# Where TensorE's unused products stand, and who adds x to the output: a planned attention and adapter kernel on one core

## Chip, cores and metric

The kernel runs on one core of a Trainium2 chip. The metric is the device time of one execution in microseconds (us). Five engines matter: TensorE (PE: matrix products, into PSUM only), VectorE (DVE), ScalarE (ACT), GpSimd (POOL) and SyncE (SP). The last two mainly issue the DMAs here. Each engine works through its own queue in order and waits on semaphores for the others.

## What is computed

The reference is a cosine-weighted linear attention followed by a mixture of eight low-rank adapters, of which each row takes two:

```
# q, k, v: 8 batches, 8 heads, 576 positions, 64 channels
phi(x) = concat(relu(x) * cos, relu(x) * sin)          # cos, sin by position
kv  = sum over s of phi(k)[s] (outer) v[s];  z = sum over s of phi(k)[s]
x   = (phi(q) @ kv) / (phi(q) @ z + 1e-6)              # then (4608 rows, 512)
logits = x @ w_gate;  top 2 of 8 experts;  w = softmax over the two
out = x + sum over the two e of w[e] * (x @ A[e]) @ B[e]
```

All inputs and the output are float32 in HBM; the kernel works in bf16 inside.

## The kernel before

**Tiling.** The 4608 rows of x are worked in 36 groups of 128 rows. A group is either 128 positions of one batch (kind "one", two j of 9) or one j of two batches (kind "two"). Batches go in four pairs; the last pair has nine groups of kind "two".

**Steps.** For each batch: load K, V and Q by DMA (`load`, L386; casting to bf16), relu of K (`relu_k`, L417), V scaled by cosine and by sine (`vscale`, L427: nine instructions on ScalarE, L434, or one on VectorE, L436), the product of K and V on TensorE (`kv_mm`, L439, 36 or 72 products, L447, into the PSUM tile pnd), and two evacuations of it into the block-diagonal tile BD (`kv_evac`, L454), one for each half of the partitions. For each group: transposes of q (`qt_mm`, L533), evacuation with relu on ScalarE (L539), times tangent on VectorE (`qt_tan`, L559), the num products (`num_mm`, L577, into pnd), a reciprocal of the denominators (L589) and the normalized tile xt (`x_xt`, L594). Then, for three groups at a time: transposes of xt (L603), their copy to SBUF (`xt_evac`), the product with A and the gate (`za_mm`, L616), the routing on VectorE and one sigmoid on ScalarE (L630 to L665), a transpose of the weighted result (L674) and its copy. The output tile of a group is summed in PSUM by two products (`dx_mm`, L682): xt times the identity (L685), which only carries x into the sum, and the routed result times B (L687). ScalarE or VectorE copies the sum to the tile osb (`osb`, L690, through `copy`, L241 or L243), and `store` (L695) sends it out from SP's or POOL's queue.

**Unused products.** TensorE also runs products whose result nobody reads. Two blocks of 18 stand at the start (`pe_warm`, L301). `pe_more` (L305 to L308) appends n products of 128x252 to a step: six to each half K·V step of batches 0 and 1 (L500) and four to the num step of the first five groups (L741), 44 in all. They write columns of pnd that the step itself leaves free.

**Order.** Nothing is scheduled at run time or by the compiler. Every step is entered in a plan (`Plan.add`) with its possible engines, their assumed costs, and the tiles that it uses. Four tables fix the rest: ORDER is the order in which all 594 steps are issued, and so each engine's queue; CHOICE picks the engine of each step; SLOTS picks the buffer of each use of a pool; HOLD makes a store wait for another DMA. Pools that matter: pnd has two buffers of two PSUM banks, shared by K·V and num; ps has four banks, shared by everything else on TensorE; osb has seven, of which the first two hold K of batch 0 at the start. The batch loads are all in POOL's queue. Waits between engines are put in by the framework, tile by tile, from what each instruction reads and writes.

Of the kernel before, what the change touches and what calls it, by code (L numbers as in the profile page):

```python
# [20 lines left out]
    26, 19, 32, 16, 20, 51, 15, 27, 14, 18, 0, 17, 1, 36, 2, 9, 29, 3, 12, 10, 52, 28, 33, 13, 31, 35, 4, 30, 11, 7,  # L21
    34, 5, 46, 37, 21, 6, 54, 50, 55, 38, 45, 39, 23, 8, 40, 44, 61, 114, 115, 41, 116, 22, 60, 125, 117, 42, 124, 43,
    126, 134, 70, 121, 127, 118, 53, 62, 122, 154, 119, 135, 120, 155, 145, 71, 144, 49, 123, 128, 69, 48, 299, 24,
    156, 131, 129, 47, 130, 298, 136, 132, 301, 133, 56, 146, 137, 79, 65, 302, 300, 57, 25, 78, 303, 58, 59, 355, 64,
    147, 141, 356, 138, 357, 360, 142, 358, 63, 80, 139, 140, 143, 304, 151, 359, 361, 305, 152, 66, 362, 88, 306, 73,
    373, 68, 74, 67, 363, 364, 148, 89, 160, 374, 161, 149, 375, 150, 171, 162, 170, 153, 307, 157, 172, 163, 308,
    376, 378, 164, 309, 158, 173, 87, 181, 159, 200, 377, 180, 201, 191, 165, 379, 166, 190, 182, 167, 380, 311, 192,
    174, 202, 183, 96, 381, 310, 72, 168, 175, 365, 169, 97, 369, 176, 177, 382, 178, 385, 193, 366, 75, 312, 179,
    107, 82, 386, 314, 393, 370, 77, 76, 313, 367, 315, 394, 187, 395, 398, 396, 184, 397, 81, 98, 83, 412, 185, 399,
    188, 186, 316, 189, 194, 400, 317, 203, 195, 413, 106, 196, 216, 217, 414, 417, 368, 197, 204, 415, 318, 416, 218,  # L30
    319, 320, 198, 418, 206, 199, 207, 321, 401, 205, 84, 105, 419, 402, 208, 219, 322, 387, 91, 383, 86, 323, 388,
    430, 209, 85, 392, 405, 384, 92, 210, 324, 420, 213, 211, 421, 406, 246, 403, 431, 247, 212, 226, 372, 227, 404,
    432, 236, 435, 90, 228, 237, 450, 433, 214, 248, 238, 93, 451, 215, 434, 452, 410, 407, 99, 95, 220, 453, 94, 455,
    229, 422, 408, 223, 221, 239, 454, 423, 424, 222, 426, 425, 390, 436, 224, 230, 437, 427, 326, 225, 438, 325, 231,
    439, 328, 456, 232, 329, 327, 233, 457, 444, 234, 330, 101, 429, 458, 440, 240, 459, 441, 235, 469, 445, 241, 446,
    100, 331, 332, 243, 333, 447, 262, 470, 263, 242, 253, 264, 252, 244, 272, 474, 471, 245, 273, 254, 102, 472, 265,
    473, 274, 255, 464, 462, 475, 110, 103, 389, 460, 463, 249, 428, 465, 476, 334, 335, 461, 250, 109, 477, 442, 478,
    466, 283, 336, 282, 487, 251, 443, 108, 479, 284, 337, 448, 488, 111, 275, 338, 492, 489, 285, 480, 483, 113, 411,
    490, 481, 104, 391, 491, 507, 112, 493, 494, 482, 256, 508, 484, 495, 509, 292, 257, 510, 486, 485, 496, 258, 259,
    293, 512, 501, 511, 260, 499, 261, 502, 266, 371, 513, 294, 500, 497, 514, 340, 506, 505, 267, 269, 268, 498, 467,  # L40
    515, 339, 270, 503, 342, 271, 341, 276, 504, 343, 344, 277, 279, 468, 516, 278, 526, 280, 281, 345, 286, 346, 527,
    347, 528, 287, 517, 529, 531, 288, 348, 449, 289, 530, 518, 543, 532, 290, 533, 349, 544, 519, 350, 291, 521, 520,
    548, 534, 545, 295, 546, 522, 535, 524, 523, 351, 547, 296, 538, 549, 352, 525, 550, 536, 409, 539, 297, 540, 537,
    551, 560, 552, 541, 353, 561, 555, 542, 354, 562, 565, 557, 563, 564, 553, 556, 566, 567, 579, 558, 554, 568, 569,
    580, 570, 559, 581, 584, 571, 582, 574, 583, 575, 572, 585, 589, 586, 573, 576, 577, 587, 588, 578, 590, 592, 591,
    593,
]
CHOICE = [
    0, 0, 0, 0, 0, 0, 0, 0, 0, 0, 0, 0, 0, 0, 0, 0, 0, 0, 0, 0, 0, 0, 0, 0, 0, 1, 0, 0, 0, 0, 0, 0, 0, 0, 0, 1, 0, 0,
    0, 0, 0, 0, 0, 1, 0, 0, 0, 0, 0, 1, 0, 0, 0, 1, 0, 1, 0, 0, 1, 0, 0, 0, 0, 0, 1, 0, 0, 0, 0, 0, 0, 0, 1, 0, 0, 0,  # L50
    0, 1, 0, 0, 0, 0, 0, 1, 0, 0, 0, 0, 0, 0, 0, 0, 0, 0, 0, 0, 0, 0, 0, 0, 0, 0, 0, 0, 1, 0, 0, 0, 0, 0, 0, 0, 0, 0,
# [4 lines left out]
    0, 0, 0, 0, 0, 0, 0, 0, 0, 0, 0, 0, 0, 0, 0, 0, 0, 0, 0, 0, 0, 0, 0, 0, 0, 0, 0, 0, 0, 0, 0, 0, 0, 0, 0, 0, 0, 1,  # L56
    0, 0, 0, 0, 0, 0, 0, 0, 0, 0, 0, 0, 0, 0, 1, 0, 0, 0, 0, 0, 0, 0, 0, 0, 0, 0, 0, 0, 0, 0, 0, 0, 0, 0, 0, 0, 0, 0,
    0, 1, 0, 0, 0, 0, 0, 0, 0, 0, 0, 0, 0, 0, 0, 0, 0, 0, 0, 0, 0, 0, 0, 0, 0, 0, 0, 0, 0, 0, 1, 0, 0, 0, 0, 0, 0, 0,
    0, 0, 1, 0, 0, 0, 0, 0, 0, 0, 1, 0, 1, 0, 0, 0, 0, 0, 0, 0, 0, 0, 0, 0, 0, 0, 1, 0, 0, 0, 1, 0, 0, 0, 0, 0, 0, 0,
    0, 0, 0, 0, 0, 0, 0, 0, 0, 0, 0, 1, 0, 0, 0, 0, 0, 0, 0, 0, 0, 0, 0, 0, 0, 0, 0, 0, 0, 1, 0, 0, 0, 0, 0, 0, 0, 0,  # L60
    0, 0, 0, 0, 0, 0, 0, 0, 0, 0, 0, 0, 0, 0, 0, 0, 0, 0, 0, 0, 0, 0, 0, 0, 0, 0, 0, 0, 0, 0, 1, 0, 0, 0, 0, 0, 0, 0,
    0, 0, 0, 0, 0, 0, 0, 0, 0, 0, 0, 0, 1, 0, 0, 0, 0, 0, 0, 0, 0, 0, 1, 0, 0, 0, 0, 0, 1, 0, 1, 1, 0, 0, 0, 0, 0, 0,
    0, 0, 0, 0, 0, 0, 0, 0, 0, 0, 0, 0, 0, 0, 0, 0, 0, 0, 0, 0, 1, 0, 0, 0, 0, 0, 1, 0, 0, 0, 0, 0, 0, 0, 0, 0, 0, 0,
    0, 0, 0, 1, 0, 0, 1, 1, 0, 0, 0, 0, 0, 0, 0, 0, 0, 0, 1, 0, 0, 0, 0, 0,
]
SLOTS = [
    2, 1, 0, 3, 0, 1, 0, 0, 0, 0, 0, 0, 1, 1, 1, 1, 0, 1, 2, 2, 2, 2, 1, 2, 3, 3, 3, 0, 0, 3, 0, 0, 4, 1, 0, 0, 1, 1,
    0, 2, 1, 1, 2, 2, 2, 0, 0, 2, 3, 3, 1, 1, 1, 3, 0, 0, 0, 1, 0, 1, 0, 1, 2, 1, 0, 2, 2, 1, 1, 3, 1, 2, 0, 2, 4, 1,
    0, 5, 0, 4, 1, 2, 6, 0, 1, 7, 3, 3, 1, 0, 8, 1, 0, 0, 2, 9, 1, 1, 10, 0, 1, 0, 0, 11, 1, 2, 12, 1, 2, 0, 1, 13, 1,
    0, 14, 3, 3, 0, 2, 15, 0, 0, 0, 0, 4, 1, 1, 2, 2, 1, 1, 2, 4, 0, 0, 1, 0, 0, 0, 1, 5, 1, 2, 3, 3, 4, 0, 0, 7, 1,  # L70
    1, 6, 1, 3, 0, 2, 8, 1, 0, 9, 1, 2, 1, 1, 10, 2, 0, 0, 2, 11, 1, 0, 14, 3, 1, 0, 1, 12, 1, 2, 2, 0, 4, 0, 0, 0, 1,
    1, 15, 0, 3, 0, 2, 13, 1, 0, 4, 1, 2, 0, 1, 5, 2, 0, 3, 1, 0, 2, 3, 3, 0, 0, 2, 1, 2, 2, 1, 3, 1, 0, 3, 1, 1, 2,
    0, 0, 2, 3, 1, 1, 0, 0, 2, 2, 1, 1, 0, 3, 0, 0, 3, 2, 2, 1, 1, 0, 0, 0, 3, 0, 2, 2, 1, 3, 2, 1, 1, 1, 1, 1, 0, 3,
    1, 3, 0, 0, 0, 0, 0, 0, 0, 4, 3, 3, 3, 1, 1, 1, 0, 1, 1, 5, 3, 1, 2, 0, 0, 0, 2, 0, 3, 6, 1, 2, 0, 1, 1, 1, 0, 1,
    0, 0, 2, 3, 1, 0, 0, 0, 3, 1, 2, 1, 1, 0, 3, 1, 1, 1, 3, 0, 1, 5, 3, 0, 2, 0, 0, 0, 3, 1, 3, 3, 3, 2, 2, 1, 1, 1,
    0, 0, 2, 1, 0, 3, 1, 0, 0, 0, 1, 1, 2, 2, 1, 3, 0, 1, 1, 1, 0, 0, 2, 5, 3, 1, 0, 0, 0, 1, 1, 0, 0,
# [3 lines left out]
    (371, 429), (389, 106), (411, 372), (449, 506),  # L80
# [65 lines left out]
def kernel(  # L146
# [86 lines left out]
    def pF(u):  # L233
        return pS[S_(u)][:, :]
# [70 lines left out]
    def pe_more(t, n):  # L305
        for _ in range(n):
            nc.tensor.matmul(out=t[:, 0, 4 * W:512], lhsT=warm[:, 0:128], rhs=warm[:, 4 * W:512], start=True, stop=True,
                             skip_group_check=True)  # L308
# [130 lines left out]
    def kv_mm(aa, uk, uvv, up, more=0):  # L439
        def f():  # L440
            kt, vt, pt = tK[S_(uk)], tVV[S_(uvv)], pND[S_(up)]
            for a in aa:
                for j in range(J):
                    for par in range(2):
                        for hh in range(2):
                            r = slice(64 * par, 64 * par + 64)
                            nc.tensor.matmul(  # L447
                                out=pt[64 * hh:64 * hh + 64, par, a * 2 * W:(a + 1) * 2 * W], lhsT=kt[r, 2 * a + hh, j, :],
                                rhs=vt[r, 2 * a + hh, j, :].rearrange("p (c w) -> p c w", c=2)[:, :, 0:W],
                                start=(j == 0), stop=(j == J - 1), skip_group_check=True)  # L450
            pe_more(pt, more)
        return f
# [20 lines left out]
    for b in range(B):  # L473
# [25 lines left out]
        for ai, aa in enumerate([[0], [1]] if b in HALF else [[0, 1]]):  # L499
            more = 6 if b in HALF else 0  # L500
            pl.add("kv", one("PE", 0.02 + 0.58 * len(aa) + 0.105 * more, kv_mm(aa, uk, uvv, upk, more)), d + 9 + ai,
                   needs=[("k", b, a) for a in aa] + [("vv", b, a, cs) for a in aa for cs in range(2)] + VCOLS,
                   makes=[("kvp", b, a) for a in aa], uses=[uk, uvv, upk, ubd], ins=72 * len(aa) + 2 * more)
# [58 lines left out]
    def num_mm(m, gs, uqt, und, more):  # L562
        g = gs[m]

        def f():
# [15 lines left out]
            pe_more(nd, more)  # L581
# [100 lines left out]
    def dx_mm(udx, uxt, uzt, i, part):  # L682
        def f():
            if part != 1:
                nc.tensor.matmul(out=pF(udx), lhsT=ident, rhs=tXT[S_(uxt)], start=True, stop=False)  # L685
            if part != 0:
# [167 lines left out]
```

## Time and profile before

| what | value |
|---|---|
| median of 13 runs | 108.7 us (107.83 to 110.24) |
| the profiled execution | 109.36 us, span 107.6 us |
| granted TensorE clock, mean | 0.989 |
| TensorE busy | 93.8 us, 87% of the span |
| VectorE busy | 87.5 us, 81% |
| ScalarE busy | 84.4 us, 78% |
| GpSimd busy | 31.4 us, 29% |
| HBM read and written | 28.85 MB and 9.44 MB |

The span runs from the first to the last instruction of the program; the rest of an execution's time lies around it. "Busy" leaves out waiting, and issuing DMAs counts only on GpSimd. A line such as L594 is a line of the kernel's file. In the profile's views `out<-in` names tiles, `x36` is a count, and a bracket such as `[0.69 <-PE pnd L307]` is how long the engine had been idle and what ended it. Where a helper records an operation (`copy`), the tile's name tells what it is.

### The profile page before, as it was taken

How to read it: one execution, taken by the hardware profiler on the slowest of the kernel's cores; microseconds unless marked ns; L12 is line 12 of the kernel's file. 1: busy time of each engine (PE TensorE's matmuls, PEld its weight loads, DVE VectorE, ACT ScalarE, POOL GpSimd, SP SyncE). 2: the span in 40 equal slices, each digit the busy share in tenths (PEclk: the TensorE clock that was granted, in tenths of full speed). 3: DMA queues.
4: the chain of work that ended last, by engine and by line, in shares of the span. 5: the costliest groups of instructions: out<-in, count | busy, mean ns of one | idle time of the engine just before them, and what ended most of it. 6: DMA issues, size and time to landing. Idle time of an engine off the chain costs nothing.

```text
span 107.6 us, 4071 instructions
## 1 busy us (share of the span) xinstructions
PE 93.8 (87%) x1717; PEld 68.7 (64%) x1728; DVE 87.5 (81%) x247; ACT 84.4 (78%) x162; POOL 31.4 (29%) x51
## 2 busy tenths in 40 slices
PE   4999997999758899979899999999999699998810
PEld 1343476888747696768678877795767378655300
DVE  5897307699879999989999799999998678896710
ACT  4639936899699699989999988999999453688710
POOL 5999682634322224222204121010001020040000
PEclk9999999999999999999999999999999999999995
DMA  2999999999999999999999999999996799889991
GB/s 78 378 201 196 191 200 203 207 196 203 207 209 209 210 205 209 208 207 211 205 209 207 207 209 208 209 208 363 351 275 181 186 273 260 309 206 301 427 397 74
DMA packets 18482, 24.71 MB, mean 230 GB/s; under 512 B 4256, under 2 KB 15648, under 8 KB 18464
## 3 DMA queue, kind: packets, MB, share of 16 engines
q0 software_dynamic: 15856, 16.59, 86.5%
q1 hardware_dynamic: 2608, 7.87, 22.5%
q8 instruction: 13, 0.21, 0.7%
q14 instruction: 5, 0.04, 0.1%
HBM read 28.85 MB, written 9.44 MB: 356 GB/s over the span
## 4 chain that ended last, share of the span: by engine, by line
PE 32%; DVE 24%; ACT 16%; DMA 12%; POOL 7%; issue 4%; ACTq 0%; DVEq 0%; POOLq 0%
ACT VV L434 9%; DMA Kb<-in_k_dram 9%; DVE xt L594 6%; PE pnd L577 6%; PE ps L616 5%; PE ps L685 5%; DVE VV L436 4%; DVE qTcs L559 4%; PE ps L603 4%; PE ps L533 4%; POOL Qb L409 4%; PE ps L687 3%; PE pnd L447 3%; DMA out_dram<-osb 3%; DVE zg L665 2%
## 5 line engine op out<-in xcount | busy, mean ns | idle before, releaser
L577 PE MATMUL pnd<-BD,qTcs 128*128 128x130 bf16 (+1 forms) x384 | 22.9, 222 | 2.5 <-ACT BD L460 1.5
L594 DVE TENSOR_TENSOR xt<-pnd,rden 128x512 bf16<-128x512 f32 x36 | 24.1, 682 | 0.2
L577 PEld LDWEIGHTS <-qTcs 128*128 128x128 bf16 (+1 forms) x384 | 18.6, 103 | 7.0 <-issue 4.5
L241 ACT COPY osb<-ps 128x512 f32<-128x512 f32 (+1 forms) x34 | 18.3, 572 | 3.1 <-remote 1.4
L539 ACT ACTIVATE qTcs<-ps 128x1024 bf16<-128x1024 bf16 (+1 forms) x20 | 18.1, 938 | 3.0 <-PE ps L533 1.8
L241 ACT COPY xT<-ps 128x1024 bf16<-128x1024 bf16 (+1 forms) x18 | 16.0, 899 | 4.3 <-PE ps L603 4.1
L436 DVE TENSOR_TENSOR VV<-Vb,TV 128x2304 bf16<-128x2304 bf16 (+1 forms) x15 | 17.0, 1143 | 0.7 <-DMA Vb<-in_v_dram 0.7
L434 ACT ACTIVATE VV<-Vb,TVf 128x128 bf16<-128x128 bf16 (+1 forms) x45 | 15.7, 435 | 1.7 <-DMA Vb<-in_v_dram 1.7
L559 DVE TENSOR_TENSOR qTcs<-qTcs,TT 128x1024 bf16<-128x1024 bf16 (+1 forms) x20 | 12.2, 620 | 5.1 <-ACT qTcs L539 5.1
L705 POOL DMA_DIRECT2D out_dram<-osb x9 | 4.8, 537 | 37.8 <-ACT osb L241 33.1
L603 PE MATMUL ps<-ident,xt 128*128 128x128 bf16 x144 | 13.2, 221 | 2.1 <-DVE xt L594 1.7
L685 PE MATMUL ps<-xt,ident 128*128 128x512 bf16 x34 | 12.9, 380 | 1.5 <-ACT sig L655 1.0
L603 PEld LDWEIGHTS <-xt 128*128 128x128 bf16 x144 | 10.0, 115 | 4.1 <-DVE xt L594 2.3
L301 PE MATMUL ps<-warm 128*128 128x512 bf16 x36 | 10.5, 458 | 1.5 <-DVE warm L295 1.5
L616 PE MATMUL ps<-AW,xT 128*128 128x136 bf16 x144 | 10.7, 223 | 0.4 <-ACT osb L241 0.4
L687 PE MATMUL ps<-Ball,zgT 128*128 128x512 bf16 x27 | 10.2, 379 | 0.6 <-DVE zgT L243 0.3
L533 PE MATMUL ps<-ident,Qb 128*64 128x128 bf16 x288 | 10.3, 221 | 0.0
L447 PE MATMUL pnd<-VV,Kb 64*64 64x130 bf16 x576 | 10.3, 219 | 0.0
L616 PEld LDWEIGHTS <-xT 128*128 128x128 bf16 x144 | 8.9, 98 | 1.7 <-issue 0.9
L533 PEld LDWEIGHTS <-Qb 128*64 128x64 bf16 x288 | 8.6, 110 | 2.1 <-issue 1.5
L589 DVE RECIPROCAL rden<-pnd 128x8 f32<-128x8 f32 x36 | 7.1, 200 | 3.4 <-PE pnd L577 2.1
L447 PEld LDWEIGHTS <-Kb 64*64 64x64 bf16 x576 | 8.7, 106 | 1.6 <-issue 0.4
(61 smaller groups left out, 118.5 us busy)
## 6 DMA issues: line engine op xcount, KB each, us to landing
Vb<-in_v_dram POOLq DMA_DIRECT2D x6, 576.0 KB, 19.0
Kb<-in_k_dram POOLq DMA_DIRECT2D x6, 576.0 KB, 19.7
Qb<-in_q_dram POOLq DMA_DIRECT2D x6, 576.0 KB, 20.2
out_dram<-osb SPq DMA_DIRECT2D x11, 256.0 KB, 6.3
out_dram<-osb SPq DMA_DIRECT2D x2, 768.0 KB, 4.7
out_dram<-osb POOLq DMA_DIRECT2D x5, 256.0 KB, 5.8
osb<-in_k_dram SPq DMA_DIRECT2D x2, 576.0 KB, 4.0
Vb<-in_v_dram POOLq DMA_DIRECT2D x4, 288.0 KB, 6.5
```

Source lines behind the costliest of these rows:

```text
L241: nc.scalar.copy(o, i)
L434: nc.scalar.activation(o[:, :, j], i[:, :, j], AF.Copy, scale=TVf[:, cs, j:j + 1])
L436: nc.vector.tensor_tensor(out=o, in0=i, in1=TV[:, cs].unsqueeze(1).to_broadcast([128, n, J, D]), op=ALU.mult)
L447: nc.tensor.matmul(out=pt[64 * hh:64 * hh + 64, par, a * 2 * W:(a + 1) * 2 * W], lhsT=kt[r, 2 * a + hh, j, :], rhs=vt[r, 2 * a + hh, j, :] ...
L533: nc.tensor.transpose(out=pt[64 * hh:64 * hh + 64, n, 2 * a:2 * a + 2, x], in_=qt[:, c, j, :], identity=ident)
L539: nc.scalar.activation(tQT[S_(uqt)][:, 0, 0:n], pB(up)[:, 0:n], AF.Relu)
L559: nc.vector.tensor_tensor(out=v[1], in0=v[0], in1=f4, op=ALU.mult)
L577: nc.tensor.matmul(out=nd[r, a, 0:4 * W].rearrange("p (h e w) -> p h e w", h=2, e=2)[:, :, par], lhsT=st, rhs=bd[:, par, a, cs].rearrange( ...
L594: nc.vector.tensor_tensor(out=tXT[S_(uxt)].rearrange("p (a h d) -> p a h d", a=2, h=4), in0=nd_view(und)[:, :, :, 0:D], in1=tRD[S_(urd)].u ...
L603: nc.tensor.transpose(out=pB(up)[:, lo:lo + 128], in_=tXT[S_(uxt)].rearrange("p (x c) -> p c x", c=4)[:, c], identity=ident)
L616: nc.tensor.matmul(out=pF(uza)[:, n * AW_W:(n + 1) * AW_W], lhsT=tXTT[S_(u)][:, k, c, :], rhs=AW[:, c, :], start=(c == 0), stop=(c == 3))
L685: nc.tensor.matmul(out=pF(udx), lhsT=ident, rhs=tXT[S_(uxt)], start=True, stop=False)
```

## The change

Three things change together, and the four tables with them.

1. `pe_more` is gone from the K·V and num steps. `pe_fill` runs unused products of the same shape, always into the first pnd buffer, ahead of the steps named in the new table FILL: 37 in six places. Step 7 is the small product of the tangent table, 118 a num group of batch 0, 135 a transpose of q of batch 1, 57 and 56 the K·V halves of batch 1, 138 a num group of batch 1.
2. The dx step of the first 33 groups gets a second form, without the identity product. With it VectorE makes the output tile by adding the PSUM sum and xt (`osb_add`). ScalarE's form is as before. In the new CHOICE seven groups take the second form.
3. ORDER, CHOICE, SLOTS and HOLD are new throughout: the order on every engine, the order of the loads, and the engine of some forty steps.

```diff
-    26, 19, 32, 16, 20, 51, 15, 27, 14, 18, 0, 17, 1, 36, 2, 9, 29, 3, 12, 10, 52, 28, 33, 13, 31, 35, 4, 30, 11, 7,
...
+    26, 0, 1, 19, 27, 29, 17, 20, 14, 45, 2, 16, 9, 23, 15, 13, 36, 10, 32, 11, 12, 28, 33, 18, 3, 37, 31, 4, 46, 51,
...
 HOLD = [
-    (371, 429), (389, 106), (411, 372), (449, 506),
+    (371, 392), (409, 98), (446, 486), (503, 504),
+]
+
+FILL = [
+    (7, 2), (118, 13), (135, 2), (57, 10), (56, 2), (138, 8),
 ]
...
-    def pe_more(t, n):
+    def pe_fill(n):
         for _ in range(n):
-            nc.tensor.matmul(out=t[:, 0, 4 * W:512], lhsT=warm[:, 0:128], rhs=warm[:, 4 * W:512], start=True, stop=True,
+            nc.tensor.matmul(out=pND[0][:, 0, 4 * W:512], lhsT=warm[:, 0:128], rhs=warm[:, 4 * W:512], start=True, stop=True,
                              skip_group_check=True)
...
-            pe_more(pt, more)
...
-            more = 6 if b in HALF else 0
-            pl.add("kv", one("PE", 0.02 + 0.58 * len(aa) + 0.105 * more, kv_mm(aa, uk, uvv, upk, more)), d + 9 + ai,
+            pl.add("kv", one("PE", 0.02 + 0.58 * len(aa), kv_mm(aa, uk, uvv, upk)), d + 9 + ai,
...
-            pe_more(nd, more)
...
-    def dx_mm(udx, uxt, uzt, i, part):
-        def f():
-            if part != 1:
+    def dx_mm(udx, uxt, uzt, i, parts):
+        def f():
+            if "x" in parts:
                 nc.tensor.matmul(out=pF(udx), lhsT=ident, rhs=tXT[S_(uxt)], start=True, stop=False)
-            if part != 0:
-                nc.tensor.matmul(out=pF(udx), lhsT=tZGT[S_(uzt)][:, i], rhs=Ball, start=False, stop=True)
+            if "d" in parts:
+                nc.tensor.matmul(out=pF(udx), lhsT=tZGT[S_(uzt)][:, i], rhs=Ball, start=parts == "d", stop=True)
         return f
...
+    def osb_add(udx, uxt, uo, i):
+        def f():
+            nc.vector.tensor_tensor(out=tOSB[S_(uo)][:, i], in0=pF(udx), in1=tXT[S_(uxt)], op=ALU.add)
         return f
...
-            more = 4 if at[g] < 5 else 0
-            pl.add("num", one("PE", (0.6 if g[0] == "two" else 0.54) + 0.105 * more, num_mm(n, gs, uqt, und, more)), dd + 1.0,
+            pl.add("num", one("PE", 0.6 if g[0] == "two" else 0.54, num_mm(n, gs, uqt, und)), dd + 1.0,
...
-                pl.add("dx", one("PE", 0.44, dx_mm(udx, uxt, uzt, i, 2)), dd + 6 + i, needs=[("zgT", key), "Ball"],
+                pl.add("dx", [("PE", 0.44, dx_mm(udx, uxt, uzt, i, "xd")), ("PE", 0.22, dx_mm(udx, uxt, uzt, i, "d"))], dd + 6 + i, needs=[("zgT", key), "Ball"],
                        makes=[("dx", g)], uses=[uxt, uzt, udx], extra=0.12, ins=4)
-                pl.add("osb", [("ACT", 0.5, osb(udx, uo, i, "ACT")), ("DVE", 0.6, osb(udx, uo, i, "DVE"))], dd + 6.4 + i,
-                       needs=[("dx", g)], makes=[("osb", g)], uses=[udx, uo])
+                pl.add("osb", [("ACT", 0.5, osb(udx, uo, i, "ACT")), ("DVE", 0.6, osb_add(udx, uxt, uo, i))], dd + 6.4 + i,
+                       needs=[("dx", g)], makes=[("osb", g)], uses=[uxt, udx, uo])
...
+        fill = dict(FILL)
         for s in order:
+            if s.idx in fill:
+                pe_fill(fill[s.idx])
             issued[s.idx] = s.emit()
```

The costs in the plan's calls (0.54, 0.105 and so on) were assumptions for choosing an order; they do nothing at run time.

## The prediction

> **What bounds the kernel now.** I read the cores' spans first (107.6 us, clock 0.989), then busy time by stretch. I cut the span where VectorE starts its first normalized tile xt (L594, 20.16) and where it ends the relu of batch 7's K (L424, 78.41):
>
> ```profile
> core 0: us, PE busy (x) PEld busy (x) DVE busy (x) ACT busy (x) POOL busy (x), PEclk, DMA share, GB/s
> 0.00:20.16 20.16, 18.06 (x200) 9.83 (x202) 11.83 (x26) 12.61 (x29) 14.94 (x26) 1.00 1.15 207
> 20.16:78.41 58.25, 53.73 (x1170) 44.01 (x1172) 55.79 (x147) 54.30 (x98) 14.31 (x22) 1.00 1.21 222
> 78.41:107.60 29.19, 21.99 (x357) 14.85 (x360) 19.89 (x76) 17.45 (x37) 2.18 (x4) 0.96 0.83 261
> ```
>
> In the middle stretch VectorE (DVE) is busy 55.79 of 58.25 us. Are the loads the bound instead? The view of the K tiles says no:
>
> ```profile
> L389 POOL DMA_DIRECT2D Kb<-in_k_dram x6: 740/742/759, 15.2 to 52.2; - x6
> DMA to landing us min/median/max: 9.2/18.9/23.6
> ```
>
> The last K load is issued at 52.2 and takes 23.6, so it lands at 75.8. VectorE reaches it at 77.66, with no wait in the timeline:
>
> ```profile
> 75.84 1.31 DVE L436 TENSOR_TENSOR VV<-Vb,TV 128x2304 bf16<-128x2304 bf16 x1
> 77.06 0.68 DVE L594 TENSOR_TENSOR xt<-pnd,rden 128x512 bf16<-128x512 f32 x1
> 77.66 0.75 DVE L424 TENSOR_SCALAR Kb<-Kb 128x2304 bf16<-128x2304 bf16 x1
> ```
>
> So VectorE's queue paces the kernel from 20 to 78 us. Before 20 it waits for TensorE (PE), whose unused products stand between a product and its reader; after 78 it alternates with PE:
>
> ```profile
> 19.02 0.21 DVE L589 RECIPROCAL rden<-pnd 128x8 f32<-128x8 f32 x1 [0.17 <-PE pnd L307]
> 19.92 0.21 DVE L589 RECIPROCAL rden<-pnd 128x8 f32<-128x8 f32 x1 [0.69 <-PE pnd L307]
> 20.16 1.29 DVE L594 TENSOR_TENSOR xt<-pnd,rden 128x512 bf16<-128x512 f32 x2
> ...
> 86.07 0.21 DVE L589 RECIPROCAL rden<-pnd 128x8 f32<-128x8 f32 x1 [0.76 <-PE pnd L577]
> ```
>
> PE looks as full (53.73 of 58.25), but its ends are modelled. The Trainium skill ("Trainium Kernel Development and Optimization", Performance Expectations) calls matmul busy time a bad metric, because matmuls are pipelined. If PE were the bound, seven fewer products would give 7 x 0.22 = 1.5 us; by the rule PE's share alone promises nothing. The back-to-back VectorE rows decide for me.
>
> **VectorE's work.** For each kind of instruction I take the distance from one start to the next where nothing waits, from before's timeline. Seven output tiles become VectorE sums; three that were VectorE copies go to ScalarE (ACT): +4 tiles at 0.65 (the copies' distance; xt, the nearest two-input row on PSUM, has 0.60) = +2.6. The sum itself is not in the trace; below it is bounded by xt's 0.60, above by its whole 0.68. One half and one full scale of V: +0.67 + 1.28. The copy of AW: +0.6 (ACT 0.86; two copies). Two xT copies: +0.9; a half output copy: +0.4. Leaving: three evacuations of BD, -2.0; a half relu, -0.3; a zgT copy, -0.25. Sum: **+3.9 to +4.1**. In queue order VectorE's work up to the first xt is 11.97 before and 12.72 after; from there through batch 7's relu 56.74 and 58.43; behind it 18.66 and 20.32. ACT loses about 7.5 us (mainly V scaling 6.3 and outputs 2.4, against evacuations 1.8 and relu 1.1), PE 1.5 of identity products and 7 of 44 unused ones (37 x 0.107 = 4.0 us instead of 4.7).
>
> **First stretch.** The program's order after: 18 unused products, 2, the small tan product, 18, K·V of the second half of batch 0's heads, 16 transposes, the large tan product, K·V of the first half, 13 unused, two num groups. VectorE has 7.1 us of work ahead of the tan product, so with its start at 0.92 this runs at 8.1; 0.3 for it and 4.0 for the 18 (9.07 to 13.06 before) give 12.5; 0.65 + 0.57 + 1.0 + 0.65 make 15.4. Batch 0's V is now loaded behind a q piece, half of batch 1's V and Gld; its last half, before issued at 3.65 and 6.5 to landing, so there at 10.1, comes near 12; its two scales (0.67 each) end at 13.4, hidden by the 14.75 at which their product can start. If the loads slipped by over 1.4 us, the rest would count.
>
> Now the point on which I weigh most: a filling product has no wait of its own in the plan, but it writes pnd0, the PSUM tile that readers have just been given. In the built program's waits the 13 stand behind ACT's evacuation of BD, the 10 behind an xt, the 8 behind an evacuation, two behind a reciprocal; two groups of 2 wait for nothing. So four of six fill after the wait, not during it. The two evacuations of BD do run one behind the other, as the trace shows for before (ACT 16.53 to 17.13, then):
>
> ```profile
> 17.17 0.71 DVE L462 CAST BD<-pnd 64x520 bf16<-64x520 f32 x1 [0.28 <-ACT BD L460]
> ```
>
> 15.5 + 0.70 + 0.05 + 0.60 = 16.9; 13 x 0.107 = 1.4 makes 18.3; two num groups at 0.47 make 19.25; reciprocals and xt at 19.65. Without that wait num would follow VectorE's tan product at about 17. Queued behind the 13: both num groups, the reciprocals and the first two xt. First xt: **0.5 us earlier**, in spite of 0.75 more work.
>
> Are the fillers needed? The granted clock is 1.00 in both first rows, and PE's longest wait between 2 and 100 us is 1.1. The Trainium skill ("TensorE: Matmul & The Clock Gate", What's actually happening) says the clock halves only after an idle window of about 3.4 us; no run here shows it. By that rule moving or dropping fillers costs no clock, and speaks against the 13.
>
> **Middle stretch.** 58.43 of work plus before's idle (58.25 - 56.74 = 1.5) plus 0.4 for the 10 and 8 fillers: 10 x 0.107 delay a K·V product that VectorE needs only later, 8 x 0.107 delay a num group that it waits for. Bounds of that: 0 (they fill a wait) and 1.9 (all 18 on its path). The relu ends at 19.65 + 60.3 = 80.0, **1.5 later**. The K load lands near 76 in either order (the same bytes in one queue, no store in SP's queue ahead of batch 6's Q), so it is covered by 4 us; without that cover nothing changes until it lands after 79.
>
> **Last stretch.** Before: 103.39 - 78.41 = 24.98, of which 18.66 is VectorE work. After: 20.32 of work. Low end: waits on PE go, what stays is the last groups' chain (sig 0.34 + 0.34, zgT, the last copies: about 2.1), 22.4. High end: the idle of 6.3 stays, 26.6. PE before had 20.4 us of work and took 4.2 more; now VectorE is the longer with 20.3, which gives 24.5 by the same margin. I take 24.1, near that row: ACT has 2.9 less here and PE 1.2. **0.9 shorter**. Four of the seven sums stand here; each can wait for a store of its output tile (ACT waited 1.35 once); the stores concerned are issued 6 us or more ahead, so I set nothing, at most 1.4. Store issues move between SP and POOL and the held ones change; the last store still follows the last copy (103.4 to 106.6 before), so the end moves with the copies.
>
> **Sum.** 80.0 + 24.1 = 104.1 against 103.39: +0.7. The profiled execution took 109.36 (span 107.6 and 1.8 around it), so 110.1 there; it lay 0.66 over the median of 108.7, so **109.4** beside the median.
>
> **Rivals.**
> 1. *The last stretch is paced by PE and ACT* (faster). For it: VectorE's waits on PE at 82 to 92 us; 1.2 us of PE and 2.9 of ACT work are gone. Against: VectorE gets 1.7 more there. With 22.4 instead of 24.1 and the fillers' 0.4 free: 80.0 - 0.4 + 22.4 = 102.0, -1.4, 107.3. It decides from a last stretch under 23.4.
> 2. *The parts cancel*: last stretch 23.4; 108.7.
> 3. *VectorE pays everywhere*: idle of the last stretch stays (26.6) or a sum waits for a store with all VectorE behind it; half of the way to 26.6 and the 1.0 left of the fillers' upper bound: +2.8, 111.5. For it: the queue is in order; against: the early stores.
> 4. *The sums do not replace products*: the program's order has 29 instead of 36 identity products and 7 sums, so no.
>
> **Chances.** Forecast 0.40 (0.33 slower by over 0.5%, 0.07 within), rival 1 0.31 (0.28 faster, 0.03 within), rival 2 0.13 (0.11 within, 0.02 faster), rival 3 0.16. 0.5% is about what a measurement can tell from no change. Faster 0.30, same 0.21, slower 0.49. Both signs hold much, so the range takes rival 1 and rival 3: 107.0 to 111.6; the forecast's own is 108.9 to 110.4.
>
> **What would show it.** VectorE busy 91 to 92 us; first xt at 19.7; the 13 fillers starting only when BD's evacuation has ended; the relu at 80.0 without a wait for its load; last copy near 104.1. I am wrong if the first xt comes before 19, if VectorE's waits on PE in the last stretch vanish, or if the granted clock falls.

## The result, and the profile after

The change made the kernel slower: **1.0146 times** the time before (95% interval 1.0105 to 1.0187), about 1.6 us. The medians are 110.76 us (11 runs, 109.44 to 112.50) and 108.63 us (48 runs, 107.83 to 111.84); the ratio leaves out executions over 1.5% above the fastest of their own kernel, of which the changed kernel has more (5 of 11, before 11 of 48), so the medians lie further apart than the ratio. The forecast was 109.4 us in 107.0 to 111.6: right in direction, and 0.9 us too small.

The two profiled executions have the same span, 107.6 us. In part this is chance: that of before (109.36 us) lies 0.7 above its median, that of the changed kernel (109.75 us) 1.0 below, and the last section shows where such a microsecond can go. In part it is the tail: the last output copy ends 1.14 us later in the changed kernel, but its last store lands 2.0 us after its issue, that of before 3.2. The last store before, then in the changed kernel (size, and us from issue to landing):

```profile
out_dram<-osb SPq DMA_DIRECT2D x1, 256.0 KB, 3.2
```

```profile
out_dram<-osb SPq DMA_DIRECT2D x1, 256.0 KB, 2.0
```

Busy time of the changed kernel by stretch, cut at the same events as before: VectorE's first xt (20.02 us) and the end of the relu of batch 7's K (81.96 us). Columns: stretch, its length, busy us and count per engine, granted clock, share of the DMA engines, GB/s.

```profile
core 0: us, PE busy (x) PEld busy (x) DVE busy (x) ACT busy (x) POOL busy (x), PEclk, DMA share, GB/s
0.00:20.02 20.02, 17.05 (x175) 9.11 (x175) 12.25 (x28) 10.76 (x27) 15.80 (x27) 1.00 1.13 201
20.02:81.96 61.94, 55.65 (x1194) 44.62 (x1194) 57.93 (x153) 52.66 (x82) 14.75 (x23) 1.00 1.20 225
81.96:107.60 25.64, 19.99 (x340) 14.05 (x345) 20.23 (x76) 14.24 (x31) 2.18 (x4) 0.96 0.87 264
```

The middle stretch is 61.94 us (before 58.25), and VectorE is idle for 4.0 of them (before 2.5). Behind it the last copy follows at 104.53 (before 103.39): that stretch lost 2.4 us (22.57 for 24.98). VectorE is busy for 90.4 us in all (forecast 91 to 92, so a little less). TensorE's timeline of the changed kernel shows the three larger groups of unused products (L311); the bracket is TensorE's wait ahead of them:

```profile
14.95 0.72 PE L451 MATMUL pnd<-VV,Kb 64*64 64x130 bf16 x36
17.10 1.56 PE L311 MATMUL pnd<-warm 128*128 128x252 bf16 x13 [1.43 <-ACT BD L463]
18.50 1.10 PE L579 MATMUL pnd<-BD,qTcs 128*128 128x130 bf16 x16
...
24.63 1.24 PE L311 MATMUL pnd<-warm 128*128 128x252 bf16 x10 [1.17 <-DVE xt L595]
25.80 0.72 PE L451 MATMUL pnd<-VV,Kb 64*64 64x130 bf16 x36
...
29.04 1.02 PE L311 MATMUL pnd<-warm 128*128 128x252 bf16 x8 [0.97 <-ACT BD L463]
29.90 1.10 PE L579 MATMUL pnd<-BD,qTcs 128*128 128x130 bf16 x16
```

TensorE stands idle for 1.43, 1.17 and 0.97 us, and only then runs the products that were meant for these gaps; the useful products come behind them. VectorE's timeline carries it on, and its last row is the relu that the prediction used as a cut, without a wait for its load (which landed at 75.87):

```profile
19.70 0.28 DVE L590 RECIPROCAL rden<-pnd 128x8 f32<-128x8 f32 x2 [1.35 <-PE pnd L579]
20.02 1.29 DVE L595 TENSOR_TENSOR xt<-pnd,rden 128x512 bf16<-128x512 f32 x2
...
30.57 0.21 DVE L590 RECIPROCAL rden<-pnd 128x8 f32<-128x8 f32 x1 [0.50 <-PE pnd L579]
31.09 0.21 DVE L590 RECIPROCAL rden<-pnd 128x8 f32<-128x8 f32 x1 [0.32 <-PE pnd L579]
...
81.22 0.74 DVE L428 TENSOR_SCALAR Kb<-Kb 128x2304 bf16<-128x2304 bf16 x1
```

### The profile page after: what moved, and what is told of

It reads as the page before. It is cut to its first block, busy times and chain, and to the rows that moved or that the text cites. A ratio compares the mean times of both kernels' runs of the same rounds, so it can differ in the third digit from the quotient of the medians.

```text
span 107.6 us, 4039 instructions
## 1 busy us (share of the span) xinstructions
PE 92.7 (86%) x1703; PEld 67.8 (63%) x1714; DVE 90.4 (84%) x254; ACT 77.7 (72%) x139; POOL 32.7 (30%) x53
## 4 chain that ended last, share of the span: by engine, by line
PE 50%; DVE 31%; issue 6%; ACT 5%; POOL 5%; DVEq 0%; POOLq 0%
PE pnd L579 12%; DVE xt L595 9%; PE pnd L451 7%; PE ps L604 5%; PE ps L617 4%; PE ps L535 4%; PE ps L686 4%; PE pnd L311 4%; PE ps L305 4%; ACT qTcs L541 3%; PE ps L688 3%; DVE VV L440 3%; DVE qTcs L561 3%; DVE osb L698 2%; DVE zg L666 2%
## 5 line engine op out<-in xcount | busy, mean ns | idle before, releaser
L440 DVE TENSOR_TENSOR VV<-Vb,TV 128x2304 bf16<-128x2304 bf16 (+1 forms) x17 | 18.9, 1137 | 2.3 <-DMA Vb<-in_v_dram 2.3
L579 PEld LDWEIGHTS <-qTcs 128*128 128x128 bf16 (+1 forms) x384 | 18.1, 103 | 3.8 <-issue 2.1
L245 ACT COPY osb<-ps 128x512 f32<-128x512 f32 (+1 forms) x29 | 15.7, 569 | 3.4 <-DVE osb L247 1.5
L245 ACT COPY xT<-ps 128x1024 bf16<-128x1024 bf16 (+1 forms) x16 | 14.9, 943 | 3.8 <-PE ps L604 3.6
L535 PE MATMUL ps<-ident,Qb 128*64 128x128 bf16 x288 | 11.1, 221 | 0.9 <-ACT qTcs L541 0.6
L686 PE MATMUL ps<-xt,ident 128*128 128x512 bf16 x29 | 10.9, 381 | 0.5 <-DVE zgT L247 0.3
L463 ACT CAST BD<-pnd 64x520 bf16<-64x520 f32 x15 | 9.0, 599 | 3.0 <-PE pnd L451 2.3
L688 PE MATMUL ps<-Ball,zgT 128*128 128x512 bf16 x25 | 9.2, 380 | 0.6 <-DVE zgT L247 0.6
```

Of the source, the lines that this page charges most:

```text
L245: nc.scalar.copy(o, i)
L440: nc.vector.tensor_tensor(out=o, in0=i, in1=TV[:, cs].unsqueeze(1).to_broadcast([128, n, J, D]), op=ALU.mult)
L535: nc.tensor.transpose(out=pt[64 * hh:64 * hh + 64, n, 2 * a:2 * a + 2, x], in_=qt[:, c, j, :], identity=ident)
L579: nc.tensor.matmul(out=nd[r, a, 0:4 * W].rearrange("p (h e w) -> p h e w", h=2, e=2)[:, :, par], lhsT=st, rhs=bd[:, par, a, cs].rearrange( ...
```

## The experiments

Three theories were put up. T1 is the prediction's: VectorE's queue paces the kernel, and the unused products cost where they end a wait of its own. T2: TensorE, with ScalarE, sets the second half. T3: the unused products matter through the granted clock (for e5 to e7, T3 is instead that the sums help by relieving ScalarE). Where each profiled execution stood, in us (start of the first, 5th and 20th xt, end of the relu of batch 7's K, end of the last output copy):

| kernel | ratio to before, interval | 1st xt | 5th | 20th | relu | last copy |
|---|---|---|---|---|---|---|
| before | 1 | 20.16 | 30.29 | 61.73 | 78.41 | 103.39 |
| changed | 1.0146 (1.0105 to 1.0187) | 20.02 | 31.22 | 62.12 | 81.96 | 104.53 |
| e8, changed again | 1.0136 (1.0058 to 1.0214) | 20.03 | 31.23 | 62.09 | 82.70 | 105.27 |
| e1, changed, no unused products | 0.9991 (0.9957 to 1.0025) | 18.64 | 28.24 | 59.14 | 79.11 | 102.38 |
| e4, changed, 13 and 8 write the free tile | 1.0024 (0.9996 to 1.0052) | 18.65 | 29.02 | 59.74 | 80.35 | 102.92 |
| e2, changed, no sums | 1.0344 (1.0310 to 1.0379) | 20.03 | 31.22 | 62.08 | 83.60 | 106.97 |
| e5, changed, 7 products back | 1.0240 (1.0176 to 1.0304) | 20.03 | 31.22 | 62.07 | 82.97 | 107.19 |
| e6, changed, more VectorE | 1.0152 (1.0070 to 1.0234) | 21.75 | 32.95 | 63.93 | 84.58 | 107.51 |
| e7, changed, more ScalarE | 1.0226 (1.0156 to 1.0296) | 20.01 | 31.21 | 62.05 | 82.91 | 106.68 |
| e3, before, no unused products | 1.0280 (1.0207 to 1.0352) | 18.26 | 30.27 | 64.32 | 82.43 | 106.47 |
| e11, before, 20 early ones gone | 0.9925 (0.9881 to 0.9968) | 18.79 | 29.67 | 61.09 | 77.79 | 102.65 |
| e9, before, 3 sums | 0.9960 (0.9926 to 0.9993) | 20.32 | 30.44 | 61.86 | 78.56 | 103.18 |
| e10, before, 7 sums | 1.0054 (1.0016 to 1.0091) | 19.58 | 30.41 | 61.78 | 79.08 | 103.28 |
| e12, before, 7 sums, early ones gone | 1.0020 (0.9982 to 1.0059) | 18.31 | 30.02 | 61.43 | 78.72 | 102.93 |

The profiled executions of one kernel can differ by 0.7 us (e8 against the first), so a row's last columns show where time went, and the ratio shows how much. The profiled executions of e3, e6 and e11 (113.18, 112.72 and 110.23 us) lie 1.0 to 1.9 us above their kernels' medians.

### The unused products: e1, e4, e3, e11

e1 empties the table:

```diff
 FILL = [
-    (7, 2), (118, 13), (135, 2), (57, 10), (56, 2), (138, 8),
 ]
```

> The changed kernel with an empty FILL table: none of the 37 unused products after the two blocks at the start; nothing that is read is left out. T1 (VectorE's queue paces the kernel; the unused products stand on its path only where they end a wait of its own): the 13 go from in front of the first num groups, so the first xt starts near 18.7 instead of 20.0, and the 8 give 0.3 to 0.8; together 1.6 to 2.1 us, ratio to the kernel before 0.995 to 1.000. T2 (the last stretch or TensorE sets the end and eats whatever is won early): first xt earlier all the same, but the ratio stays at 1.010 to 1.015. T3 (the unused products are needed for TensorE's clock): granted clock under 0.95 in a row of the first stretch and a ratio over 1.02.

e4 keeps all 37 and lets two groups write the other pnd buffer:

```diff
-    def pe_fill(n):
+    def pe_fill(n, p):
...
-            nc.tensor.matmul(out=pND[0][:, 0, 4 * W:512], lhsT=warm[:, 0:128], rhs=warm[:, 4 * W:512], start=True, stop=True,
+            nc.tensor.matmul(out=pND[p][:, 0, 4 * W:512], lhsT=warm[:, 0:128], rhs=warm[:, 4 * W:512], start=True, stop=True,
...
-                pe_fill(fill[s.idx])
+                pe_fill(fill[s.idx], 1 if s.idx in (118, 138) else 0)
```

> The changed kernel with the groups of 13 and of 8 unused products writing the second pnd buffer, which nobody reads at that time, instead of the first: they then wait for nothing and run while ScalarE evacuates BD. As many unused products as before. T1: the 13 start at 15.6 instead of 17.1 and are done when the evacuation ends, first xt 18.7 to 18.9; ratio as in the kernel without fillers within 0.003 (0.996 to 1.003). T2: first xt earlier, ratio still 1.010 to 1.015. If it is the number of unused products and not their place that costs, the first xt stays at 20.0.

Both came out as T1 had it: 0.9991 and 1.0024. TensorE's timeline of e4:

```profile
14.98 0.72 PE L451 MATMUL pnd<-VV,Kb 64*64 64x130 bf16 x36
15.64 1.57 PE L311 MATMUL pnd<-warm 128*128 128x252 bf16 x13
17.14 1.10 PE L579 MATMUL pnd<-BD,qTcs 128*128 128x130 bf16 x16
```

The same 13 products now start right behind K·V, at 15.64 instead of 17.10, and num follows when the evacuation has ended, at 17.14 instead of 18.50. The first xt is 1.37 us earlier, the 5th 2.20, the last copy 1.61, and the ratio falls by 0.012, or 1.3 us. Nothing but the written buffer differs, so **the place of the unused products, set by the tile that they write, costs about 1.3 of the change's 1.6 us**. Leaving all out gives 0.3% more (1.7 us in all), which the two intervals do not separate.

e3 and e11 ask the same of the kernel before. e3 sets `more` to 0 in both places; e11 keeps those of batch 1 and of the later num groups:

```diff
-            more = 6 if b in HALF else 0
+            more = 6 if b == 1 else 0
-            more = 4 if at[g] < 5 else 0
+            more = 4 if 2 <= at[g] < 5 else 0
```

> The kernel before without its 44 appended unused products (the two blocks at the start stay); nothing that is read is left out. T1: VectorE's two waits for them before its first xt (0.17 and 0.69) and those behind it go, first xt 0.5 to 1.3 us earlier than 20.16, ratio 0.988 to 0.997. T2 (the end is set elsewhere): 0.997 to 1.003. T3 (they keep TensorE's clock): granted clock under 0.95 in the first stretch, ratio over 1.01.

> The kernel before without those of its unused products that stand ahead of its first normalized tiles (12 in batch 0's K.V, 8 in the first two num groups); the 24 behind them stay, so that TensorE's longest waits at 20 to 30 us are filled as before. If they cost what the run without any of them showed (first xt 18.3 instead of 20.2) and the clock holds: ratio 0.982 to 0.990 if it is carried to the end, 0.994 to 1.000 if a load or TensorE's later work takes it back. If the clock falls as in the run without any: over 1.01, and a row at 0.5 near 30 us.

e3 reached its first xt 1.9 us earlier and lost it all: 1.028. T3's signs came here, a ratio over 1.01 and a lower clock (not in the first stretch, as T3 had it, but behind it), and the prediction's view that dropping unused products costs no clock was wrong for this order. TensorE's timeline of e3, then its stretches:

```profile
22.59 0.42 PE L603 MATMUL ps<-ident,xt 128*128 128x128 bf16 x4 [1.88 <-DVE xt L594]
...
26.73 0.89 PE L616 MATMUL ps<-AW,xT 128*128 128x136 bf16 x12 [2.08 <-ACT AW L241]
```

```profile
26.00:28.00 2.00, 0.89 (x12) 0.84 (x13) 2.00 (x4) 0.89 (x4) 1.22 (x2) 1.00 1.21 206
28.00:30.00 2.00, 1.48 (x16) 1.21 (x15) 1.73 (x9) 1.98 (x5) 0.74 (x1) 0.74 1.21 207
30.00:32.00 2.00, 0.98 (x10) 0.98 (x11) 1.52 (x4) 2.00 (x6) 0.48 (x1) 0.50 1.22 210
34.00:36.00 2.00, 2.00 (x51) 1.82 (x44) 1.72 (x2) 0.90 (x2) 0.74 (x1) 0.55 1.21 205
36.00:38.00 2.00, 2.00 (x47) 1.65 (x44) 1.22 (x7) 1.14 (x3) 0.69 (x1) 1.00 1.21 209
```

Behind waits of 1.88 and 2.08 us the granted clock is 0.50 from about 29 to 35 us (the mean over the span is 0.95 to 0.965 in five of its six executions, 0.995 in the sixth); between the 5th and the 20th xt e3 loses 2.6 us against the kernel before. The sixth execution, whose clock held, still took 110.6 us, 1.8 over the median of the kernel before on the same chip (108.8), so the clock need not be all of it; one execution does not say what the rest is. e11 keeps the products that fill those waits and drops the 20 in front of the first xt: clock 1.00 in these rows, and 0.9925, the lowest ratio of all, between the two ranges expected for a clock that holds. So in this order unused products are worth their time in a gap, and cost time in front of a reader; in the changed order all 37 could go without loss (e1).

### The sums: e2, e9, e10, e12

e2 sets the fourteen CHOICE entries of the seven sums (424 and 425, 440 and 441, and so on to 553 and 554) from 1 to 0.

> The changed kernel with the seven VectorE sums taken back: each group has its identity product again and ScalarE copies the sum. VectorE loses 7 x 0.65 = 4.6 us of work, 2.0 before the relu of batch 7's K and 2.6 behind it; TensorE gains 1.5, ScalarE about 4.2. T1 (VectorE's queue paces): the relu of batch 7's K ends 1.5 to 2.0 us earlier than in the changed kernel (81.96), the last stretch gets 0 to 1 shorter; ratio 0.99 to 1.00. T2 (TensorE and ScalarE set the last stretch): the relu comes earlier by up to 2.0 but the last stretch gets longer by as much or more, ratio 1.010 to 1.025. T3 (clock): no difference from the changed kernel, 1.0146.

It took 4.6 us of work from VectorE and became **slower by 2%**: 1.0344. T1's forecast (0.99 to 1.00) failed, and T2's (1.010 to 1.025) was exceeded: to the 20th xt nothing differs, then the relu comes 0.9 us later than in e8, and the last stretch takes 0.8 more (23.37 for 22.57). The sums are not what costs; they save about 2.1 us. Since e2 also gives ScalarE 4.2 us and TensorE 1.5, it does not say by itself which engine sets the pace; e5 to e7 below ask that.

For the kernel before, e9 takes over the change's two forms of dx and its `osb_add`, and chooses them for the three whole tiles that VectorE copies there; in e10 four groups that ScalarE copied follow (CHOICE 440 and 441, 497 and 498, 499 and 500, 517 and 518 to 1).

```diff
-                pl.add("dx", one("PE", 0.44, dx_mm(udx, uxt, uzt, i, 2)), dd + 6 + i, needs=[("zgT", key), "Ball"],
+                pl.add("dx", [("PE", 0.44, dx_mm(udx, uxt, uzt, i, 2)), ("PE", 0.22, dx_mm(udx, uxt, uzt, i, 3))], dd + 6 + i, needs=[("zgT", key), "Ball"],
```

> The kernel before, in its own order, with its three whole output tiles that VectorE copies (groups one/1/3, two/5/8, two/7/5) made by VectorE as sums: three identity products fewer on TensorE (0.66 us), nothing moved between engines. T2, as it stands after the first eight runs (TensorE paces the second half; about three quarters of a microsecond per microsecond of its work reach the end): -0.4 to -0.7 us, ratio 0.993 to 0.997. T1 (VectorE's queue paces): 0.999 to 1.002, as the sum takes VectorE as long as the copy.

> The same, and four more groups (one/2/3, one/4/3, one/5/0, one/5/2) go from ScalarE's copy to VectorE's sum: TensorE 1.5 us less than in the kernel before, ScalarE 2.3 less, VectorE 2.6 more, three of the four behind 85 us. T2: -1.0 to -1.6 us, ratio 0.985 to 0.991. T1: +1 to +2.6 us, ratio 1.01 to 1.024.

e9 gave 0.9960, as T2 had it: three products less, 0.4 us (the interval just reaches T1's 0.999). e10, which T2 wanted faster still (0.985 to 0.991), gave 1.0054, nearer to T1's 1.01: four more sums cost 1.0 us against e9. VectorE's timelines around the first of the four, e9 and then e10:

```profile
67.93 1.30 DVE L436 TENSOR_TENSOR VV<-Vb,TV 128x2304 bf16<-128x2304 bf16 x1
69.16 0.68 DVE L594 TENSOR_TENSOR xt<-pnd,rden 128x512 bf16<-128x512 f32 x1
```

```profile
67.86 1.30 DVE L436 TENSOR_TENSOR VV<-Vb,TV 128x2304 bf16<-128x2304 bf16 x1
69.08 0.68 DVE L692 TENSOR_TENSOR osb<-ps,xt 128x512 f32<-128x512 f32 x1
69.68 0.68 DVE L594 TENSOR_TENSOR xt<-pnd,rden 128x512 bf16<-128x512 f32 x1
```

The sum moves xt, and all that VectorE does up to 85 us, by its full 0.60 (from 0.08 ahead to 0.52 behind). In that order VectorE's queue does pace this stretch, as the prediction said of it. T2 as a rule for both orders falls too. These two profiled executions do not show the ratio's 1.0 us at the end: the last copies are 0.1 apart (103.28 and 103.18). e9's TensorE has a stall of 0.58 at 84 us that e10's has not (last section), which may be part of the reason.

> The kernel before with both: seven VectorE sums and no unused products ahead of its first normalized tiles. T2: the gains of the two add, less what the last K load (75.8 us) takes back: ratio 0.970 to 0.985. T1: 1.00 to 1.01.

e12 joins e10 and e11: 1.0020. T2's gain (0.970 to 0.985) did not come; the two added would give 0.9979, which the interval (0.9982 to 1.0059) hardly tells apart. Of the 1.85 us that its first xt is ahead, 0.3 is left at the 20th: VectorE now waits at 20.0 us for a load of V (0.40), at 21.5 for one of K (0.23), and at 24.3 for ScalarE's evacuation of qTcs (0.84), where the kernel before waits 0.21 in all up to 26 us.

### One engine a little more: e5, e6, e7, e8

Each gives one engine a little more at the seven sums of the changed kernel. The aim was 1.5 us; by the distance from one start to the next, e5 gives TensorE 1.5 (7 x 0.22), e6 gives VectorE 2.2 (0.92 instead of 0.60 each time), and e7 gives ScalarE about 2.1 (0.78 instead of 0.48). e5 puts the identity product back and lets VectorE copy; e6 repeats each sum on 128 columns; e7 repeats seven of ScalarE's neighbouring copies on 128 columns; e8 is the changed kernel itself.

```diff
-... ("PE", 0.22, dx_mm(udx, uxt, uzt, i, "d")) ...
+... ("PE", 0.44, dx_mm(udx, uxt, uzt, i, "xd")) ...
...
-... ("DVE", 0.6, osb_add(udx, uxt, uo, i)) ...
+... ("DVE", 0.6, osb(udx, uo, i, "DVE")) ...
```

> The changed kernel, but the seven VectorE groups have their identity product again and VectorE copies the sum instead of adding: TensorE has 7 x 0.22 = 1.5 us more, VectorE and ScalarE what they have in the changed kernel. T1 (VectorE's queue paces from 20 us to the end, as the prediction had it): ratio as the changed kernel's, 1.012 to 1.017. T2 (TensorE paces from 50 us on, and the sums' gain is the product saved): +1.5 us, ratio 1.026 to 1.031. T3 (what the sums save is ScalarE's 4 us): 1.012 to 1.017. This is to be read beside e8, the changed kernel on the same chip.

```diff
             nc.vector.tensor_tensor(out=tOSB[S_(uo)][:, i], in0=pF(udx), in1=tXT[S_(uxt)], op=ALU.add)
+            nc.vector.tensor_tensor(out=tOSB[S_(uo)][:, i, 0:128], in0=pF(udx)[:, 0:128], in1=tXT[S_(uxt)][:, 0:128], op=ALU.add)
```

> The changed kernel with each of the seven VectorE sums followed by the same sum once more on 128 of its 512 columns, some 0.2 us each: VectorE has about 1.5 us more at the very places where e5 gives TensorE 1.5 more. T1: +1.5 us over the changed kernel, ratio 1.026 to 1.031. T2: 0 to 0.5, ratio 1.013 to 1.019. T3: the same as T2.

```diff
             copy(eng, tOSB[S_(uo)][:, i, lo:hi], pF(udx)[:, lo:hi])
+            if again:
+                copy(eng, tOSB[S_(uo)][:, i, 0:128], pF(udx)[:, 0:128])
```

> The changed kernel with seven of ScalarE's output copies, each the one nearest ahead of a VectorE sum, followed by a copy of 128 of the columns once more, some 0.25 us each: ScalarE has about 1.7 us more. T1 and T2: 0 to 0.4, ratio 1.012 to 1.018. T3: +1 to +1.7, ratio 1.024 to 1.031.

> The changed kernel itself, on the chip of the three above and with a second profile. All theories: ratio 1.011 to 1.019. If its profiled execution lies nearer to its median (110.8) than the first one (109.75) did, the two traces show where an ordinary execution loses the last microsecond: the theory of a lost clock expects a row under 0.95, the theory of waiting engines expects the same milestones up to 60 us and a longer last stretch.

e8's profiled execution, 110.46 us, is 0.7 longer than the first one of the same program; the two agree to 74 us, no row of either is under 0.95 before the last, and the difference is one stall (last section), so neither a lost clock nor a longer last stretch. Against e8's 1.0136: TensorE's extra work cost 1.0% (1.1 us), VectorE's 0.2%, ScalarE's 0.9%. The intervals are 0.6 to 0.8% to each side and all overlap, so the ratios only suggest that TensorE weighs more than VectorE, and the rest is read from one trace of each. In e5 the last stretch is 24.22 for 22.57; 0.75 of that is a gap with a stall of another kind in it (0.56, last section), and the remaining 0.9 is what four products take (4 x 0.22). In e7 a like stall takes 0.53 of the 1.4 that its last copy is behind, so ScalarE's share is at most 0.9 and stays open. In e6 the first xt is 1.72 late for a reason of the clock (below) and the last copy 2.24 late: 0.5 for 2.2 us of VectorE work. **In these traces of the changed kernel TensorE's work reaches the end in full behind 83 us, VectorE's by a quarter.**

## Why the prediction was right, and where it was wrong

**The fillers: right, and undersized.** They stood behind the waits that the prediction read from the built program; the 13 began at 17.10 (forecast 16.9) when BD's evacuation had ended, and cost 1.37 us at the first xt (from e4; forecast 1.4). The first xt came at 20.02, not 19.65: the evacuation 0.2 later, and from num's start to VectorE's reciprocal 1.20, not 0.94. The step "0.4 for the 10 and 8 fillers" failed by size: moving the 8 alone gave another 0.83 at the 5th xt, and dropping the 10 and the twos 0.78 more (e1 against e4). That K·V product is not "needed only later": batch 1's last BD evacuation ends at 27.65 in e4 and at 26.62 in e1.

**The middle stretch: the step that failed.** "58.43 of work plus before's idle (1.5) plus 0.4" gave +1.5 at the relu; it came 3.55 later. The work was as planned and the sum's 0.65 held (0.60 from start to start, 0.67 whole, no wait in its row). The idle was 3.5, not 1.9 (4.0 by busy time): 2.0 of it lie between 20 and 32 us (0.8 is the fillers', as e4 has 1.2 there), the rest in waits of about 0.3, mostly on TensorE, as at 48.8, 60.3 and 66.9 us; the one at 48.8 follows a stall of TensorE of the kind in the last section. The premise behind it, that VectorE's queue alone paces 20 to 78 us, is shown for the order of before from 69 to 85 us (e10) and fails there near 20 to 25, where a head start went into waits for loads and ScalarE (e12). It does not hold for the new order, where taking 4.6 us off VectorE and giving work to the other two made it slower (e2), and 2.2 us more on VectorE cost 0.5 (e6). A rearranged order has its own bound; the prediction carried the old one over.

**The last stretch: rival 1's mechanism, not its result.** It took 22.57, not 24.1: VectorE's waits on TensorE all but vanished (10 us from 85 to 95: 9.38 busy, before 7.89), which the prediction had named as a sign of being wrong, and 22.57 is under rival 1's deciding 23.4. Two things hid this. The 4.2 us by which the prediction let TensorE fall behind its own work in the old stretch held 1.0 that was no wait on an engine: the row that the profile puts down to a sigmoid.

```profile
84.40 0.82 PE L685 MATMUL ps<-xt,ident 128*128 128x512 bf16 x2 [1.02 <-ACT sig L655]
```

In e9 the idle time there is 0.58, in e10, whose program up to there has two products fewer than before, none. And the work that TensorE (1.2 us) and ScalarE (2.9) no longer had here was priced at 0.4 in all, though e5 shows that the identity products alone, four here or 0.9 us, count in full.

**The sum.** The errors (+0.4 at the first xt, +1.6 behind it, -1.5 in the last stretch) nearly cancel: last copy 104.53 for 104.1 in the profiled execution, so the good sum is luck. "The end moves with the copies" missed the tail: the last store lands in 2.0 us instead of 3.2, in seven of the eight profiles of the changed order (e1 2.8), and in 3.0 to 4.8 in the six of the order before; why is not shown. Against the measured ratio the forecast was 0.9 short; the two profiled executions, which differ by 0.4 us where the ratio says 1.6, do not show where that part lies. Rival 3's terms add up to 3.0, not 2.8, and what is left of the fillers' bound of 1.9 is 1.5, not 1.0; nothing else rests on this.

**The clock.** "Moving or dropping fillers costs no clock" held in e1 (one execution of twelve had a mean clock under 0.98, 0.958) and failed in e3 and in one profile of e6 (last section). **K's load** was covered, and the **stores** held no sum up.

**What the change is made of**, from e4 and e2 by difference: fillers behind waits +1.3 us, sums -2.1, so the new tables with neither would be some 2.4 us slower than before. This last term is arithmetic and takes the parts to add, which no run tested here; no run has these tables alone. What in the new order costs it stays open. One candidate is in the traces: TensorE's stalls of 0.3 us or more between 40 and 100 us (last section) come to 0.4 to 1.9 us in the eight profiles of the new order and to 0 to 1.0 in five of the six of the old one (e3: 2.4). e11 and e9 beat both kernels (0.9925, 0.9960); the two together were not run.

## What to carry to other kernels

A filling product runs in a gap only if it waits for nothing itself: look at which buffer it writes and who last read that, and give it one that nobody uses. Before pricing moved work by the engine that looks fullest, add a microsecond to each engine in turn, check in the trace how much was really added, and see which reaches the end; after an order is rearranged, ask again. Here a sum that took the place of a copy on the same engine was free (0.67 us for 0.68), and one that moved to a queue without waits delayed that queue by its full 0.60.

## What the runs showed of the hardware

**The clock can fall after a wait of 1.43 us.** In e6's profiled execution TensorE had the same wait ahead of the 13 fillers as in the five other profiles of the changed order with these fillers in place, and there the clock fell. Its timeline, then its stretches:

```profile
17.19 2.85 PE L311 MATMUL pnd<-warm 128*128 128x252 bf16 x13 [1.43 <-ACT BD L463]
19.82 1.51 PE L579 MATMUL pnd<-BD,qTcs 128*128 128x130 bf16 x16
```

```profile
16.00:17.00 1.00, 0.00 (x0) 0.00 (x0) 1.00 (x2) 0.47 (x1) 0.60 (x1) 1.00 1.44 218
18.00:19.00 1.00, 1.00 (x7) 0.70 (x6) 0.44 (x1) 0.00 (x0) 0.00 (x0) 0.50 1.21 204
```

The fillers took 2.85 us instead of 1.56, and the first xt came at 21.75 instead of 20.03. Fillers behind a wait do not only fail to guard the clock: they then run at half speed in front of the useful work. In those five, and in e1, where num follows it, the same wait left the clock at 1.00. The Trainium skill ("TensorE: Matmul & The Clock Gate", What's actually happening) puts the fall behind an idle window of about 3.4 us that runs freely. The waits here (1.43; 1.88 and 2.08 in e3) are shorter, so if that rule holds, a window can count as idle without being so throughout: in the 3.4 us up to 17.2 e6's TensorE was busy for 1.97. How often this happens was not counted.

**TensorE's code is loaded while it runs, and sometimes comes late.** The changed kernel and e8 are the same program and agree within 0.3 us up to 74 us. Then, the changed kernel first and e8 below:

```profile
73.88 0.61 PE L604 MATMUL ps<-ident,xt 128*128 128x128 bf16 x8
74.33 0.64 PE L579 MATMUL pnd<-BD,qTcs 128*128 128x130 bf16 x8
```

```profile
73.91 0.44 PE L604 MATMUL ps<-ident,xt 128*128 128x128 bf16 x5
74.88 0.36 PE L604 MATMUL ps<-ident,xt 128*128 128x128 bf16 x3 [0.52 <-issue]
```

In the middle of eight equal transposes e8 stands still for 0.5 us and waits for nothing that the profile shows; from there it is 0.74 behind to the end. The DMA rows of e8's page have a queue for code:

```profile
q8 instruction: 13, 0.21, 0.7%
```

These are 13 packets of 16 KB. Counted over all of TensorE's recorded instructions, the unexplained stalls of e6 stand at numbers 1473, 1729 and 2492, that of e5 at 3000, that of before (the row above) at 3001: 256, then about 3 x 256 and 2 x 256 apart. e1, which has 74 weight loads and products fewer ahead, stalls at 3001 as e7 does, so 74 instructions further on in the program.

The packets' own times in the traces bear it out. For the place at 74 us the code packet runs from 71.39 to 72.45 in the changed kernel and from 72.58 to 73.52 in e8. Over all 14 profiles there are 26 such stalls of 0.3 to 1.6 us between 40 and 100 us, and each ends 1.25 to 1.65 us after a packet of this queue has ended; by that measure the changed kernel's block was ready by 74.1, as TensorE reached it, and e8's not before 74.8. In the kernel before the row put down to a sigmoid ends 1.38 us after such a packet; in e10 the packet comes 0.4 earlier, and nothing stops. No run moved a packet by itself, and what delays one is not shown.

The Trainium skill ("Runtime: NRT & Kernel Launch", Instruction fetch mechanics) says that code comes in 16 KiB blocks of 256 instructions over a DMA queue of the engine's own, ahead of need, and is mostly hidden; spacing and packets agree, the hiding does not always: 0.3 to 1.6 us show, in one execution and not in the next.
